# A linear-attention block in front of a feed-forward block: another order and another place of the sums for the products that make keys, values and queries

## The chip, the cores and the metric

The kernel runs on one core of a Trainium2 chip. The metric is the device time of one execution in microseconds (us). PE is TensorE (matmuls), DVE is VectorE, ACT is ScalarE, POOL is GpSimd, and SP is the engine whose queue issues all transfers (DMA) of this kernel. Each engine works through its own instructions in order and stops at the first one whose inputs or buffers are not ready.

## The reference

All arrays are float32: 2048 tokens (S), width 576 (D), 32 heads of 18 channels, feed-forward width 4608.

```python
xn = layernorm(x)                                   # per token, no weights
q, k, v = split(xn @ wqkv)                          # per head: 18 channels each
phi = lambda t: where(t > 0, t + 1, exp(t)) + 1e-6
pq, pk = phi(q), phi(k)
kv = einsum("bhsd,bhse->bhde", pk, v)               # one 18 x 18 state per head
z  = einsum("bhsd->bhd", pk)
num = einsum("bhqd,bhde->bhqe", pq, kv)
den = einsum("bhqd,bhd->bhq", pq, z)[..., None] + 1e-6
s = (num / den) @ wo
g = silu(gelu(xn @ w1 + b1) @ w2 + b2)
out = x + s * g
```

## The kernel before

**Precision.** Float32 products are made of three matmuls each on a pair of parts: a *high* part (a cast, on ACT) and a *low* part (the number minus its high part, on DVE or POOL): high times high, high times low, low times high.

**Tiles and pairs.** The tokens are 16 tiles of 128; two tiles make a pair p, 0 to 7. In the transposed x, a pair and its contraction halves form a 2 x 2 block matrix, and so do the weights of q, k, v. Seven products of sums of blocks (numbered 1 to 7, `product_x`, matmuls at L344) replace the eight plain block products; a rest of the contraction (`REST_OF`) is added to four of them. One product writes 2 x 432 columns (288 for keys or values and 144 for queries in each half) in a double bank of PSUM (`bank2`; there are three of them).

**Start.** The first four tiles are normalized and transposed on PE. Pair 0 is made by four plain products, one for each tile and column half (`plain_x`: 14 steps of two matmuls). The raw weights come in ten loads; their casts (`split_w`, L302 and L303) and the four sums of weight blocks that the seven products need (`w_sum`, L310: T3, T2 and T4 on POOL, T1 on DVE; casts at L315 and L319) are spread over the work of pairs 0 and 1. From pair 2 on, x arrives already transposed from memory (`load_xt`), the token statistics are broadcast through memory (`share_stats`, `load_stats`), POOL subtracts the means (`center`, L239), DVE scales (`scale`, L243) and adds blocks (`x_sums`, L249 to L254), ACT casts (`x_hi_ops`, L257) and DVE makes low parts (`x_lo_ops`, L261). The operands of all pairs are also stored in memory (`store_ops`, tensor `x_dram`, L275) for the feed-forward part.

**Pairs 1 to 7** (`phase1_pair`, `pair`, `evict`). The products run in the order 1, 2, 6, 7, 5, 4, 3. Product 1 is copied to `u` by ACT (L731); 6 is added to it by DVE (L734), 7 is added to that into a second `u` (L736), and the results of 5, 4 and 3 are each added to one of the two (L396, L403, L746). Product 2 accumulates on top of product 1, and 3 on top of 5. The keys go through `phi_hi` (three ACT passes, L373 to L375) and `phi_max` (one DVE pass, L378), and so do the queries of the pair before. `state(p - 1)` (L418) adds the pair before to the sums over tokens, ten matmuls after product 1. Work for the next pairs hangs on the products as hooks (`after1`, `after2`, ...). For the last two pairs only keys and values are made first (N = 288); their queries follow (`pair(..., "q")`), because the final state is then needed sooner.

**Rounds.** Operands of the feed-forward weights are prepared once and stored: five rounds of `we` and nine of `w2`. A round loads, then sums on POOL (L452 and L453, L482), casts on ACT (L459, L486), makes low parts on DVE (L463, L490), stores, and loads the next one. `whole_round` does it in one go: one in each of pairs 2 to 5, two in each of pairs 6 and 7, and one in each of the first turns of attention.

**Attention.** `wo` is folded into the state (`fold_wo`, L958). Then a loop over 16 query tiles, in order `TO`: sums with POOL (L907), denominators on DVE (L914 to L918), the quotient on POOL (L922), a transpose on PE (L1011), a cast, and 28 matmuls (`attend`, L1066). Beside it, x is read back from `x_dram` for the first half of the tokens (`load_x_part`, L1273, four transfers for each segment).

**Feed-forward.** Eighteen steps, nine for each half of the tokens (L1378, L1517). In the last step of the first half, x of the second half is loaded (`load_x_next`).

Engines follow the written order of the program from the first tile to the end of attention (`in_order`).

Of the kernel before, what the change touches and what calls it, by code (L numbers as in the profile page):

```python
# [15 lines left out]
P = 128  # L16
S = 2048
D = 576
# [29 lines left out]
def linear_attention_gated_ffn(ctx, tc, x, xT, wqkv, wo, w1, w1e, b1, w2, b2, out):  # L48
# [52 lines left out]
    b1c = pers.tile([P, NF], F32, name="b1c")  # L101
    nhalf = cst.tile([P, 1], F32, name="nhalf")
    nc.gpsimd.memset(nhalf, -0.5)
    tiny = cst.tile([P, 1], F32, name="tiny")
    nc.gpsimd.memset(tiny, 1e-6)
# [4 lines left out]
    x_dram = dram.tile([2, QH, P, 28, P], F32, name="x_dram")  # L110
# [38 lines left out]
    ORDER_X = (1, 2, 6, 7, 5, 4, 3)  # L149
# [34 lines left out]

    def statistics(t):
# [3 lines left out]
        mv = t0.tile([P, 4], F32, tag="mv", name=f"mv{t}", bufs=4)  # L189
        nc.vector.bn_aggr(mv[:, 0:2], st)  # L190
        nc.vector.tensor_scalar_add(mv[:, 2:3], mv[:, 1:2], 1e-5)
        nc.gpsimd.tensor_tensor(mv[:, 1:2], mv[:, 2:3], nhalf, op=ALU.pow)
        stats[t] = mv
# [80 lines left out]
    def store_ops(p):  # L274
        nc.sync.dma_start(x_dram[p // QH, p % QH], OPS[p].bitcast(F32))  # L275
# [70 lines left out]
    def product_x(p, i, ps, part, first):  # L346
# [4 lines left out]
        if i in REST_OF:  # L351
            r, n = REST_OF[i]
            seq += [(XR[p][:, r], t[:, n]) for t in W["R"]]
        for n, (st, mv) in enumerate(seq):
            mm(ps, st, mv, part, first and n == 0, n == len(seq) - 1)

    def plain_x(j, n, ps, order):

        hi = ((10, 11, 12, 13), (2, 3, 0, 1))[j]
        for i, s in enumerate(order):  # L360
            k = int(s[2])
            if k == 4:
                st = XR[0][:, (REST_T0, REST_T1)[j]]
            else:
                st = OPS[0][:, hi[k] + XLO * (s[0] == "l")]
            mm(ps, st, w_plain(k, n)[s[1] == "l"], "all", i == 0, i == len(order) - 1)
# [45 lines left out]
    def state(p):  # L412
        if not ps_kv:
            ps_kv.extend((bank1("ps_kva"), bank1("ps_kvb")))
        for j in (1, 0):
# [7 lines left out]

    def phi_k1_hi(p):
        phi_hi(f"k{p}1", as2(k_bufs[1]))

    def phi_k1_max(p):
        phi_max(f"k{p}1", k_bufs[1], as2(k_bufs[1]))
# [12 lines left out]
    class W2Round:  # L441
# [9 lines left out]
        def sums(self):  # L451
            nc.gpsimd.tensor_tensor(self.src[5][0], self.src[5][1], self.src[5][0], op=SUB)  # L452
            nc.gpsimd.tensor_tensor(self.src[6][0], self.src[6][0], self.src[6][1], op=SUB)  # L453
# [16 lines left out]
    class WeRound:  # L470
# [8 lines left out]
        def sums(self):  # L479
            u = self.u  # L480
            for dst, a, b in ((4, 0, 1), (5, 3, 0), (6, 3, 4), (7, 2, 6)):
                nc.gpsimd.tensor_tensor(u[:, dst], u[:, a], u[:, b], op=SUB)  # L482
# [25 lines left out]
    def round_sums():  # L508
        loaded[0].sums()
# [11 lines left out]
    def whole_round():  # L521
        if loaded:
            round_sums(), round_hi(), round_lo(), round_store()

# [5 lines left out]
    xn_all = opp.tile([P, 4 * KT * P], F32, tag="OPS", name="xn")  # L530
    r_tile(0), op_tiles(0), r_tile(1)
    for t in range(4):
        xn[t] = xn_all[:, t * KT * P : (t + 1) * KT * P]
# [8 lines left out]
    load_x(3)  # L542
# [5 lines left out]
    def transpose_into(t, places):  # L548
        for k, dst in enumerate(places):
            nc.tensor.transpose(dst, xn[t][:, k * P : (k + 1) * P], ident)  # L550

    def slots(ps, n=4):
        return ps[:, : n * P].rearrange("p (k c) -> p k c", k=n)

    FIRST = "hh0 hh1 lh0 lh1 hl0 hh2 lh2 hl1 hh3 lh3 hl2 hh4 hl3 hl4".split()
    LATER = "hh2 lh2 hl2 hh3 lh3 hl3 hh0 lh0 hl0 hh1 lh1 hl1 hh4 hl4".split()
    assert sorted(FIRST) == sorted(LATER)
    dve, pool = nc.vector, nc.gpsimd

    statistics(0)  # L560
    normalize_dve(0)
    split_w(0, 0, dve)
    split_w(1, 0, pool)

    ta, tb = bank1("pt0a"), bank1("pt0b")
    a4, b1_ = slots(ta), slots(tb, 1)[:, 0]
    transpose_into(0, [a4[:, k] for k in range(4)] + [b1_])
    o0, xr0 = OPS[0], XR[0]
    nc.scalar.copy(xr0[:, REST_T0], b1_)
    for k in (slice(0, 2), slice(2, 4)):  # L570
        h, l = o0[:, 10 + k.start : 10 + k.stop], o0[:, 24 + k.start : 24 + k.stop]
        nc.vector.tensor_copy(h, a4[:, k])
        nc.vector.tensor_tensor(l, a4[:, k], h.bitcast(F32), op=SUB)
    nc.vector.tensor_tensor(
        xr0[64:, REST_T0], b1_[64:], xr0[64:, REST_T0].bitcast(F32), op=SUB
    )
    split_w(2, 0, pool)
    split_w(3, 0, dve)
    split_w(4, 0, dve)
    statistics(1)  # L580
    offset(1)
    xa = bank2("x00")
    plain_x(0, 0, xa, FIRST)
    normalize_act(1)

    pt1 = bank2("pt1")
    c4, d1 = slots(pt1[:, 0]), slots(pt1[:, 1], 1)[:, 0]
    transpose_into(1, [c4[:, 2], c4[:, 3], c4[:, 0], c4[:, 1], d1])
    split_w(2, 1, dve)
    split_w(3, 1, dve)  # L590
    nc.scalar.copy(o0[:, 0:4], c4)
    nc.scalar.copy(xr0[:, REST_T1], d1)
    nc.vector.tensor_tensor(o0[:, 14:18], c4, o0[:, 0:4].bitcast(F32), op=SUB)
    nc.vector.tensor_tensor(
        xr0[64:, REST_T1], d1[64:], xr0[64:, REST_T1].bitcast(F32), op=SUB
    )
    xc = bank2("x02")
    plain_x(1, 0, xc, FIRST)
    statistics(2)
    offset(2)  # L600
    q_tile(0)
    phi_hi("k00", kv_of(xa))
    copy_q(0, 0, xa)
    phi_max("k00", k_bufs[0], kv_of(xa))
    normalize_act(2)
    nc.scalar.copy(R[0][:, 13:17], a4)
    nc.scalar.copy(R[0][:, 17], b1_)
    split_w(0, 1, dve)
    split_w(1, 1, dve)
    split_w(4, 1, dve)  # L610
    load_x(4), load_x(5)

    def transpose_to_r(t):
        pa, pb = bank1(f"pt{t}a"), bank1(f"pt{t}b")
        if t % 2:
            a, b = slots(pa, 3), slots(pb, 2)
            transpose_into(t, [a[:, 0], a[:, 1], b[:, 0], b[:, 1], a[:, 2]])
            return (R[1][:, 0:3], a), (R[1][:, 3:5], b)
        a, b = slots(pa), slots(pb, 1)
        transpose_into(t, [a[:, k] for k in range(4)] + [b[:, 0]])  # L620
        return (R[1][:, 13:17], a), (R[1][:, 17:18], b)

    to_r = transpose_to_r(2)
    statistics(3)
    offset(3)
    w_sum("T3", 0, pool), w_sum("T3", 1, pool)
    for dst, src in to_r:
        nc.scalar.copy(dst, src)
    normalize_act(3)
    xa = bank2("x01")  # L630
    plain_x(1, 1, xa, LATER)

    q_tile(1)
    phi_hi("k01", kv_of(xc))
    copy_q(1, 0, xc)
    phi_max("k01", k_bufs[1], kv_of(xc))
    memset_v()
    nc.scalar.copy(R[0][:, 3:5], c4[:, 0:2])
    nc.scalar.copy(R[0][:, 0:2], c4[:, 2:4])
    nc.scalar.copy(R[0][:, 2], d1)  # L640
    w_sum("T1", 0, dve), w_sum("T1", 1, dve)
    for k in range(2):
        w_sum("T2", k, pool), w_sum("T4", k, pool)
    x_sums(0, rest=False)
    store_rest(0)
    to_r = transpose_to_r(3)
    for dst, src in to_r:
# [1250 lines left out]
```

## Time and profile before

| | |
|---|---|
| two runs | 1268.87 and 1269.29 us, median 1269.08 |
| the profiled execution | 1267.1 us, of it the span of the profile 1265.4 |
| PE busy | 1129.8 us (89%) in 6480 matmuls |
| DVE busy | 856.0 us (68%) |
| ACT busy | 502.8 us (40%) |
| POOL busy | 481.9 us (38%) |
| mean granted clock of PE | 0.932 |
| transfers | 284.94 MB in 120784 packets, mean 225 GB/s |

The span runs from the first to the last instruction. The granted clock is the share of full speed that PE was given. A wait in brackets, "[12.43 <-DVE kph L378]", is the idle time of the engine ahead of an instruction, and what ended it: an instruction by its engine, the tile that it writes, and its line. A timeline row gives start, length, engine, line, operation, output<-inputs, sizes and count.

### The profile page before, as it was taken

The numbers are of one execution on the slowest core, as the hardware profiler recorded it, in microseconds if no ns is written. First come the engines' busy times: TensorE is split into PE (matmuls) and PEld (weight loads), VectorE is DVE, ScalarE is ACT, GpSimd is POOL, SyncE is SP. The second block draws the span as 40 slices with busy tenths as digits, with TensorE's granted clock in tenths as the row PEclk, the third lists the DMA queues.
The fourth block names the chain that finished last, engine by engine and source line by source line (L and its number), as shares of the span: only waits on it lengthen the run. The fifth ranks groups of instructions, "written<-read, shape, count | busy, mean of one in ns | idle before, by whom it ended". The sixth has DMA issues, their size and how long they took to land.

```text
span 1265.4 us, 17904 instructions
## 1 busy us (share of the span) xinstructions
PE 1129.8 (89%) x6480; PEld 1034.5 (82%) x6480; DVE 856.0 (68%) x1221; ACT 502.8 (40%) x835; POOL 481.9 (38%) x410
## 2 busy tenths in 40 slices
PE   8687998556558599999999999979999999999998
PEld 7577897555557588998998998878999899899888
DVE  6856776236445188888888888875576567557666
ACT  5543554234223154455445445425234223323333
POOL 2423222213454254455545445533134223423430
PEclk8688898777778799999999999999999999999999
DMA  5256655423789996568568657799776667777552
GB/s 197 83 206 202 210 180 230 163 70 101 238 269 298 308 375 244 189 263 297 209 217 319 221 191 283 252 303 380 264 258 208 223 204 241 231 215 234 165 158 105
DMA packets 120784, 284.94 MB, mean 225 GB/s; under 512 B 13558, under 2 KB 55542, under 8 KB 118136
## 3 DMA queue, kind: packets, MB, share of 16 engines
q1 hardware_dynamic: 120696, 283.80, 65.7%
q8 instruction: 51, 0.84, 0.3%
q14 instruction: 37, 0.30, 0.1%
HBM read 176.23 MB, written 106.64 MB: 224 GB/s over the span
## 4 chain that ended last, share of the span: by engine, by line
PE 65%; DMA 6%; SPq 3%; DVE 3%; ACT 2%; POOL 1%; issue 1%; POOLq 0%; DVEq 0%; ACTq 0%
PE pm L1517 29%; PE zy L1378 9%; PE e L1378 9%; PE a L1378 9%; PE b L1378 5%; PE pd L1637 2%; DMA w2r<-w 1%; SPq L1273 1%; PE xq L344 1%; DMA q<-q_dram 1%; PE ps_s L1066 1%; DMA rq_dram<-wa_rest0s 1%; DMA rxm<-rq_dram 1%; DMA we<-we_dram 0%; PE ps_kw L958 0%
## 5 line engine op out<-in xcount | busy, mean ns | idle before, releaser
L1523 DVE TENSOR_TENSOR macc<-pm,macc 128x576 f32<-128x576 f32 x218 | 163.9, 752 | 49.9 <-PE pm L1517 48.4
L1101 ACT CAST h_h<-g 128x512 fp32r<-128x512 f32 x204 | 121.8, 621 | 132.7 <-PE pm L1517 131.7
L1104 DVE TENSOR_TENSOR h_l<-g,h_h 128x512 fp32r<-128x512 f32 x204 | 161.8, 800 | 0.0
L1483 POOL TENSOR_TENSOR mid<-g 128x512 f32<-128x512 f32 x34 | 43.9, 1291 | 120.2 <-ACT g L1386 120.2
L1477 POOL TENSOR_TENSOR g<-g 128x512 f32<-128x512 f32 x34 | 54.9, 1615 | 50.1 <-DVE h_l L1104 28.2
L1386 ACT ACTIVATE g<-b,b1c 128x512 f32<-128x512 f32 x36 | 24.9, 690 | 105.3 <-DVE b L1404 105.3
L1395 ACT COPY mid<-a 128x512 f32<-128x512 f32 x36 | 21.1, 585 | 111.1 <-PE a L1378 111.1
L1398 DVE TENSOR_TENSOR mid<-b,mid 128x512 f32<-128x512 f32 x36 | 24.8, 690 | 55.0 <-PE b L1378 52.2
L1147 POOL TENSOR_TENSOR w1raw<-w1raw 128x256 f32<-128x256 f32 x18 | 13.2, 736 | 124.9 <-ACT h_h L1101 68.2
L463 DVE TENSOR_TENSOR w2o<-w2r,w2o 128x576 fp32r<-128x576 f32 x18 | 24.1, 1337 | 53.7 <-ACT w2o L459 52.6
L1480 POOL TENSOR_TENSOR g<-g 128x512 f32<-128x512 f32 x34 | 55.2, 1623 | 2.7
L1066 PE MATMUL ps_s<-kw_h,th 128*128 128x288 f32 x160 | 42.6, 354 | 13.4 <-ACT kw_h L1054 7.0
L1608 POOL TENSOR_TENSOR fin1l<-fin1h,fin1l 128x288 f32<-128x288 f32 x8 | 7.0, 875 | 118.8 <-DMA fin1l<-s_dram 55.5
L1378 PE MATMUL a<-h0r,wa 128*128 128x512 f32 x144 | 50.4, 390 | 0.0
L1378 PE MATMUL a<-h0f,wa 128*128 128x512 f32 x144 | 50.4, 390 | 0.0
L1104 DVE TENSOR_TENSOR h_l<-mid,h_h 128x512 fp32r<-128x512 f32 x34 | 48.8, 1435 | 1.2
L418 PE MATMUL ps_kva<-kph,vb 128*127 128x126 f32 x128 | 26.1, 368 | 25.6 <-DVE kph L378 21.2
L1011 PE MATMUL ptp<-ident,vb 128*128 128x128 f32 x80 | 15.8, 338 | 34.5 <-ACT s L1071 22.4
L418 PEld LDWEIGHTS ps_kva<-kph,vb 128*127 128x127 f32 x128 | 23.2, 271 | 27.8 <-DVE kph L378 23.2
L1386 ACT ACTIVATE g<-e,b1c 128x512 f32<-128x512 f32 x36 | 24.8, 689 | 51.2 <-DVE e L1411 51.2
L1474 POOL TENSOR_TENSOR g<-g 128x512 f32<-128x512 f32 x34 | 44.0, 1295 | 2.7
L1066 PEld LDWEIGHTS ps_s<-kw_h,th 128*128 128x128 f32 x160 | 31.8, 234 | 16.1 <-ACT kw_h L1054 7.4
(998 smaller groups left out, 3715.3 us busy)
## 6 DMA issues: line engine op xcount, KB each, us to landing
we<-we_dram SPq DMA_DIRECT2D x36, 448.0 KB, 6.0
x_dram<-OPS SPq DMA_DIRECT2D x8, 1792.0 KB
w2raw<-w SPq DMA_DIRECT2D x10, 1152.0 KB
op<-w2o SPq DMA_DIRECT2D x18, 576.0 KB, 3.9
w1raw<-w SPq DMA_DIRECT2D x18, 512.0 KB, 5.8
op_a<-wa SPq DMA_DIRECT2D x18, 512.0 KB, 5.5
op_c<-wc SPq DMA_DIRECT2D x18, 512.0 KB, 4.1
op_d<-wd SPq DMA_DIRECT2D x18, 512.0 KB, 5.6
```

The costliest lines, as they stand in the source:

```text
L418: nc.tensor.matmul(dst, v_bufs[j][:, i, : G + 1], k_bufs[j][:, g : g + n], start=(p == 0 and j == 1 and i in (0, 4)), stop=(p == NPR - 1 a ...
L1066: nc.tensor.matmul(ps[:, h, :HD], st[:, k, :], w[:, k, h * HD : (h + 1) * HD], start=(i == 0), stop=(i == len(seq) - 1),)
L1101: nc.scalar.copy(pair[0], src)
L1104: eng.tensor_tensor(pair[1], src, pair[0].bitcast(F32), op=SUB)
L1378: nc.tensor.matmul(ps, st, mv, start=first and n == 0, stop=n == len(seq) - 1, skip_group_check=True,)
L1386: nc.scalar.activation(g, ps, AF.Gelu_apprx_tanh, bias=b1c[:, f : f + 1])
L1474: tt(src[5, pr], A(1, 0), A(1, 1), op=ADD)
L1477: tt(src[6, pr], src[5, pr], A(0, 0), op=SUB)
L1480: tt(src[3, pr], A(0, 1), src[6, pr], op=SUB)
L1483: tt(src[7, pr], A(0, 0), A(1, 0), op=SUB)
L1517: nc.tensor.matmul(ps[:, q, :HD], hs[p][st][:, cs], m[:, p, :], start=(n == 0 and i not in CHAIN), stop=(n == 5), skip_group_check=True,)
L1523: nc.vector.tensor_tensor(dst, src, dst, op=ADD)
```

## The change

- **Pair 1 is plain too:** pairs 0 and 1 are made by four plain products each (`plain_x` takes the pair), and the seven products start with pair 2. The first four tiles go from their transposes straight to operands. Queries of tiles 0 to 3 are stored without phi, which is applied in attention (`RAW`). All weight sums are on POOL.
- **Four products in one tile:** the order is 2, 1, 6, 7, 5, 4, 3. Products 1, 6, 7 and 4 accumulate in one PSUM tile A; ACT copies A after 1, 6 and 7 (`snapshot`). The DVE additions into `u` are gone. The rest products of 2 and 5 are steps of their own (`e2`, `e5`), and the state of the pair before is split in two halves (`sa`, `sb`) between the products. T1's keys and queries come out of A without an addition; those of T0 now need one.
- **Rounds:** one in each of pairs 3 to 7 and one in the queries of pair 6, with sums, casts, low parts and store on different hooks. In attention a round takes two turns: sums, now on DVE, at the end of an even turn, the rest at the end of the next. Six rounds lie ahead of attention (eight before) and eight in it (six before).
- **x by partition:** `x_dram` holds 512 tokens in a row for each partition and segment. A pair stores 512-byte pieces; a segment is read in one transfer instead of four.
- **Around the state:** phi of the first two query tiles, the fold and the first denominators hang on other products of the last part; phi of the last two query tiles moves into the second turn of attention; a copy (`zb`) moves from ACT to POOL.

```diff
-    x_dram = dram.tile([2, QH, P, 28, P], F32, name="x_dram")
+    x_dram = dram.tile([2, P, 28, 512], F32, name="x_dram")
...
-    ORDER_X = (1, 2, 6, 7, 5, 4, 3)
+    ORDER_X = (2, 1, "e2", "sa", 6, "sb", "e5", 7, 5, 4, 3)
...
     def store_ops(p):
-        nc.sync.dma_start(x_dram[p // QH, p % QH], OPS[p].bitcast(F32))
+        cs = slice(p % QH * P, (p % QH + 1) * P)
+        nc.sync.dma_start(x_dram[p // QH, :, :, cs], OPS[p].bitcast(F32))
...
+    x10 = bank2("x10")
+    plain_x(1, 0, 0, x10, THEN[:10], last=False)
+    transpose_x(3)
+    plain_x(1, 0, 0, x10, THEN[10:], first=False)
...
+    w_sum("T4", 0, pool), w_sum("T4", 1, pool)
+    k10 = phi_plain(2, x10)
+    state(0)
+    x12 = bank2("x12")
+    plain_x(1, 1, 0, x12, THEN)
+    k10()
+    scale(2)
+    x_sums(2)
+    w_hi("T2", 0), w_hi("T2", 1)
+    w_lo("T2", 0, dve), w_lo("T2", 1, dve)
...
+    x13 = bank2("x13")
+    plain_x(1, 1, 1, x13, THEN)
...
+    x11 = bank2("x11")
+    plain_x(1, 0, 1, x11, THEN)
...
-        elif i == 6:
-            u = u_part(u1, part)
-            nc.vector.tensor_tensor(u, ps_part(ps, part), u, op=ADD)
-        elif i == 7:
-            nc.vector.tensor_tensor(
-                u_part(u2, part), ps_part(ps, part), u_part(u1, part), op=ADD
-            )
...
+    def snapshot(p, n, ps, part):
+        nc.scalar.copy(u_part(u_all[p][n], part), ps_part(ps, part))
+
+    def products(p, part, hooks, before=None):
...
+        for i in ORDER_X:
+            if i == 2:
+                X0 = bank2(f"x0{part}{p}")
+                product_x(p, 2, X0, part, True, rest=False)
+            elif i == 1:
+                A = bank2(f"xa{part}{p}")
+                product_x(p, 1, A, part, True)
+                snapshot(p, 0, A, part)
+            elif i == "e2":
+                rest_alone(p, 2, X0, part, False)
+            elif i in ("sa", "sb"):
+                if before is not None:
+                    state(before, (1,) if i == "sa" else (0,))
+            elif i == 6:
+                product_x(p, 6, A, part, False, rest=False)
+                snapshot(p, 1, A, part)
+            elif i == "e5":
+                X1 = bank2(f"x1{part}{p}")
+                rest_alone(p, 5, X1, part, True)
+                u = u_all[p][0]
+                if kv:
+                    nc.vector.tensor_tensor(
+                        as2(k_bufs[0]), kv_of(X0), as2(u)[:, :, :KV], op=ADD
+                    )
+                    phi_hi(f"k{p}0", as2(k_bufs[0]))
+                if q:
+                    add_q(T0, 0, X0, u, part)
+            elif i == 7:
+                product_x(p, 7, A, part, False, rest=False)
+                snapshot(p, 0, A, part)
+                if kv:
+                    phi_max(f"k{p}0", k_bufs[0], as2(k_bufs[0]))
+            elif i == 5:
+                product_x(p, 5, X1, part, False, rest=False)
+                if kv:
+                    add_v(1, X1, u_all[p][0])
+                if q:
+                    add_q(T1, 1, X1, u_all[p][0], part)
+            elif i == 4:
+                product_x(p, 4, A, part, False)
+                if kv:
+                    phi_hi(f"k{p}1", kv_of(A))
+                if q:
+                    copy_q(T1, 0, A, part)
+            else:
+                product_x(p, 3, X1, part, False)
+                def end():
+                    if kv:
+                        phi_max(f"k{p}1", k_bufs[1], kv_of(A))
+                        add_v(0, X1, u_all[p][1])
+                    if q:
+                        add_q(T0, 1, X1, u_all[p][1], part)
+                pend.append(end)
             hooks.get(i, lambda: None)()
...
-    ROUND_OF = {2: 1, 3: 1, 4: 1, 5: 1, 6: 2, 7: 2}
...
+        def h1():
+            if steady:
+                operands_hi()
...
+            if p in ROUNDS:
+                round_sums()
...
+        def hsb():
+            if steady:
+                operands_lo()
+            if first:
+                w_hi("T4", 0), w_hi("T4", 1)
+                w_lo("T4", 0, pool), w_lo("T4", 1, pool)
+                center(3)
+            if p in ROUNDS:
+                round_hi()
...
+        def h7():
+            if nxt and not first:
+                center(nxt)
+            if first:
+                operands()
+                operands_hi()
+            if p in ROUNDS:
+                round_lo(), round_store()
...
-    pair(NPR - 2, "q", {})
+    products(NPR - 2, "q", {2: round_sums, 7: lambda: (round_hi(), round_lo(), round_store())})
...
         for a, n, to in X_SEGS[k]:
-            for c in range(QH):
-                nc.sync.dma_start(
-                    t[:, to : to + n, c * P : (c + 1) * P].bitcast(F32),
-                    x_dram[half, c, :, a : a + n],
-                )
+            nc.sync.dma_start(t[:, to : to + n].bitcast(F32), x_dram[half, :, a : a + n])
...
         if j + 4 < NT:
+            if TO[j + 4] in RAW:
+                phi_q_hi(TO[j + 4]), phi_q_max(TO[j + 4])
             by_sums(j + 4)
             denominators(j + 4)
             p_mult(j + 4)
+        if j == 1:
+            for t in TO[-2:]:
+                phi_q_hi(t), phi_q_max(t), store_q(t)
         beside(j)
-        if j < 9 and loaded:
-            whole_round()
+        if loaded and j % 2 == 0:
+            round_sums(dve)
+        elif loaded:
+            round_hi(), round_lo(), round_store()
```

More of the change, by code (lines that the diff above doesn't have):

```diff
@@ L344, in mm, with product_x @@
             nc.tensor.matmul(dst, st, w, start=start, stop=stop, skip_group_check=True)
-    def product_x(p, i, ps, part, first):
+    def product_x(p, i, ps, part, first, rest=True):
         (wh, wl), a, o = W[W_OF[i]], X_OF[i], OPS[p]
@@ L561, in linear_attention_gated_ffn @@
     normalize_dve(0)
-    split_w(0, 0, dve)
+    split_w(0, 0, pool)
+    transpose_x(0)
     split_w(1, 0, pool)
[L565 to L573, printed above, removed]
@@ new lines, in linear_attention_gated_ffn @@
+    for k in (2, 3, 4):
+        if k == 2:
+            statistics(1)
+        split_w(k, 0, dve)
+        if k == 2:
+            offset(1)
+    x00 = bank2("x00")
+    plain_x(0, 0, 0, x00, FIRST[:12], last=False)
+    normalize(1)
+    transpose_x(1)
+    plain_x(0, 0, 0, x00, FIRST[12:], first=False)
+    ones_of_v()
+    statistics(2), offset(2)
+    tile_hi(1)
+    tile_lo(1)
+    split_w(2, 1, dve), split_w(3, 1, dve)
+    x02 = bank2("x02")
+    plain_x(0, 1, 0, x02, THEN)
+    k00 = phi_plain(0, x00)
```

456 lines of the change are left out of this document (225 added, 231 removed).

## The prediction

> **What bounds the kernel now.** I read the page, then one table of stretches, then the waits of PE, then the timeline round the gaps.
>
> ```profile
> span 1265.4 us, 17904 instructions
> 0.00:45.00 45.00, 35.37 (x152) 31.82 (x153) 29.30 (x43) 22.96 (x41) 19.40 (x23) 0.85 0.38 140
> 45.00:85.00 40.00, 29.11 (x121) 26.59 (x120) 28.78 (x51) 19.87 (x29) 10.59 (x8) 0.74 0.50 185
> 85.00:121.00 36.00, 27.31 (x125) 25.29 (x124) 21.06 (x40) 12.87 (x19) 10.57 (x12) 0.81 0.54 171
> 121.00:195.00 74.00, 69.42 (x359) 64.72 (x358) 53.48 (x102) 38.05 (x55) 22.02 (x20) 0.95 0.65 221
> 195.00:249.00 54.00, 37.04 (x244) 36.32 (x243) 24.84 (x39) 19.84 (x28) 11.65 (x28) 0.81 0.46 168
> 249.00:290.00 41.00, 25.10 (x141) 22.65 (x140) 13.00 (x25) 12.34 (x23) 5.58 (x4) 0.79 0.29 92
> 290.00:304.00 14.00, 4.74 (x22) 2.82 (x20) 9.89 (x19) 8.61 (x17) 6.22 (x5) 0.69 0.26 85
> 304.00:380.00 76.00, 48.12 (x259) 44.03 (x258) 38.81 (x53) 18.44 (x36) 36.65 (x28) 0.77 0.71 235
> 380.00:442.00 62.00, 42.99 (x265) 40.91 (x265) 23.77 (x44) 15.51 (x31) 20.65 (x17) 0.81 0.95 303
> 442.00:826.00 384.00, 383.47 (x2246) 348.28 (x2247) 332.74 (x433) 185.45 (x321) 201.19 (x163) 1.00 0.71 256
> 826.00:854.00 28.00, 21.02 (x151) 20.35 (x151) 20.08 (x25) 7.65 (x11) 8.50 (x6) 0.96 1.05 296
> 854.00:1265.00 411.00, 406.09 (x2412) 370.71 (x2411) 260.19 (x353) 141.25 (x228) 128.91 (x100) 0.99 0.68 222
> ```
>
> The columns are the stretch, its length, the busy time of PE, PE's weight loads, DVE, ACT and POOL, the granted clock, the DMA share and GB/s. I cut the table where the kernel changes work: plain products of pair 0 until 45, pair 1 until 85, pair 2 until 121, pairs 3 to 5 until 195, keys and values of pairs 6 and 7 until 249, their queries until 290, the start of attention, attention until 442, then the feed-forward part. From 442 on PE is full but for 826 to 854, so only the first 442 us and that one hole can shrink. There PE is idle about a quarter of the time, and the clock is low wherever it is idle.
>
> ```profile
> PE ps_kva L418 <- DVE kph L378: 21.2, 6, 12.4
> PE xq L344 <- ACT u L731: 15.9, 2, 11.3
> PE ptp L1011 <- ACT s L1071: 22.4, 5, 6.5
> 232.92 2.07 PE L418 MATMUL ps_kva<-kph,vb 128*127 128x126 f32 x8 [12.43 <-DVE kph L378]
> 261.19 0.61 PE L344 MATMUL xq<-wB21h,OPS 128*128 128x288 f32 x1 [11.28 <-ACT u L731]
> 276.55 0.61 PE L344 MATMUL xq<-wB21h,OPS 128*128 128x288 f32 x1 [4.62 <-ACT u L731]
> 224.80 1.40 POOL L452 TENSOR_TENSOR w2r<-w2r 128x576 f32<-128x576 f32 x1 [20.34 <-DMA w2r<-w]
> ```
>
> The waits (total, times, longest) have one source behind several names. A round of w2 is done in one go: POOL waits for the load, then ACT, DVE and the store follow, and each engine stops in order. POOL starts a sum the moment its load lands (224.80), PE resumes at 232.92; 11.28 and the waits for s in attention are the same picture.
>
> **The change part by part.** First the prices.
>
> ```profile
> 8.08 2.78 PE L344 MATMUL x<-wB11h,OPS 128*128 128x432 f32 x8 [1.38 <-DVE OPS L572]
> 123.92 1.15 PE L418 MATMUL ps_kva<-kph,vb 128*127 128x126 f32 x8 [0.64 <-DVE kph L378]
> 126.16 0.64 PE L344 MATMUL xall<-wB21h,OPS 128*128 128x432 f32 x2
> 129.38 0.56 PE L344 MATMUL xall<-wT2h,OPS 128*128 128x432 f32 x2
> 131.75 0.56 PE L344 MATMUL xall<-wT3h,OPS 128*128 128x432 f32 x2
> 239.43 0.43 PE L344 MATMUL xkv<-wT2h,OPS 128*128 128x288 f32 x2
> 241.02 0.43 PE L344 MATMUL xkv<-wT3h,OPS 128*128 128x288 f32 x2
> 125.05 0.88 ACT L731 COPY u<-xall 128x864 f32<-128x864 f32 x1 [1.98 <-DVE q L403]
> 132.25 1.05 DVE L734 TENSOR_TENSOR u<-xall,u 128x864 f32<-128x864 f32 x1
> 37.81 9.32 POOL L310 TENSOR_TENSOR raw<-raw,raw 128x864 f32<-128x864 f32 x4 [2.00 <-DVE raw L310]
> 40.91 2.15 DVE L250 TENSOR_TENSOR R<-R 128x256 f32<-128x256 f32 x1
> 126.92 0.43 DVE L250 TENSOR_TENSOR R<-R 128x256 f32<-128x256 f32 x1
> 273.87 0.68 ACT L373 ACTIVATE eq<-q 128x576 f32<-128x576 f32 x1
> ```
>
> Twelve matmuls take 131.75 − 129.38 = 2.37 us, 0.1975 each; keys and values alone 1.59, 0.1325 each; the state's ten 126.16 − 123.92 = 2.24.
>
> *Start.* Pair 1 is now plain: 8 products of 28 matmuls, 224 × 0.1975 = 44.2, with one state 46.5. At the clock of the first stretch, 0.85, that is 54.7; the first product starts at 8.1, which makes 63. I add 8 of waits: PE was idle 45 − 35.4 = 9.6 before. All eight sums of weights lie on POOL now (9.32 / 4 = 2.33 each, 18.6) beside the sums of x on DVE, which take 2.15 there and 0.43 with POOL free. So pair 2 starts at 71 instead of 85: **−14**. Bounds: 55 (full clock, no wait) and 85.
>
> *Pair 2* takes over the weights' casts, and what it hands to pair 3 goes through POOL twice (low parts of T4, then centering) before DVE may scale. Floor 100 × 0.1975 + 2.24 = 22; pair 1 with this work took 40. I take 31, near the middle, against the 36 of today's pair 2: **−5**.
>
> *Pairs 3 to 5.* DVE loses two adds of 1.05, ACT gains two copies of 0.88 (busy 38.05 of 74 now). The copy is a new wait: PE may not go on in that bank before it, and queued behind it on ACT are the operand casts, for which DVE's low parts wait. Rest products and half of the state, 0.8 + 1.1 = 1.9 us, lie between; they cover 0.88 if ACT comes in time. Floor 3 × 22 = 66, now 74 with PE busy 69.4. I take 72: **−2**; bounds 66 and 80.
>
> *Pairs 6 and 7.* Floor 2 × (13.25 + 2.24) = 31, now 54. One round per pair, its sums, casts and store in three places, loses the 12.4 and most of the rest of 21.2. I take 37: **−17**; bounds 31 and 54.
>
> *Queries of 6 and 7.* Both waits, 11.28 + 4.62, are for a copy behind other ACT work; the first goes with the round, but the exponentials of two query tiles now stand ahead of copies of pair 7, as today. I take **−10**; bounds 0 and −16. *290 to 304* keeps its chain of casts: 0, with ±2.
>
> *Attention.* Rounds are split over two turns, so POOL and PE stop less. But DMA was busy 0.71 × 76 + 0.95 × 62 = 113 us of the 138, and two rounds more fall into this stretch.
>
> ```profile
> x_dram<-OPS SPq DMA_DIRECT2D x8, 1792.0 KB
> op<-w2o SPq DMA_DIRECT2D x18, 576.0 KB, 3.9
> w2r<-w SPq DMA_DIRECT2D x9, 864.0 KB, 6.4
> we_dram<-weo SPq DMA_DIRECT2D x5, 896.0 KB, 4.5
> 825.00:850.00 25.00, 21.64 (x158) 20.97 (x156) 20.32 (x26) 7.65 (x11) 9.50 (x6) 1.00 1.06 281
> 850.00:855.00 5.00, 1.38 (x3) 1.16 (x4) 0.00 (x0) 0.55 (x2) 0.00 (x0) 0.67 1.01 406
> 853.62 0.80 PE L1378 MATMUL a<-rxm,we 128*128 128x512 f32 x1 [6.98 <-DMA we<-we_dram]
> ```
>
> One round of each kind is about 864 + 2 × 576 + 896 KB and a small load, 3.2 MB, 8 us at 406 GB/s. Against it, half of x, 4 × 1792 KB = 7.3 MB, is read in long rows instead of 512-byte pieces: 25 to 27 us at the 281 GB/s of 825 to 850, where such pieces run, 18 at 406. The two cancel; 113 at a share of 0.95 is 119. I take 122: **−16**; bounds 113 and 138 + 8 = 146. The exponentials of query tiles 0 to 3 move here, and those of the last two, with their stores, from ahead of attention into its second turn. Each is three ACT passes of 0.68, so 2 us; they cost nothing while ACT is busy only 18.44 of 76. Without that cover it would be 12. On SP the round's stores and its next load now stand behind a turn's load of x and ahead of the next turn's store of s; a late round would hold that store, and with it the next load of queries.
>
> The Trainium skill, DMA: Bandwidth & Descriptors, section Specifications, puts the smallest transfer at line rate at 512 B. By it the new layout would bring no speed, only fewer issues, and the attention term would be −8. The trace differs: both windows above are full, at 281 and 406.
>
> *Half change.* At 853.62 PE has waited 6.98 for a load queued behind x. 7 MB (281 GB/s for 25 us) land about 8 us sooner at 406, and ten issues replace forty on SP: **−7**; bounds 0 and −9. The price stands in the stores, now 512-byte rows: 8 × 1.8 MB, 2 us more each, 16 in all, hidden while the DMA share stays at 0.65 and below until 290; 16 if that cover were gone.
>
> Sum: 14 + 5 + 2 + 17 + 10 + 16 + 7 = 71. The profiled execution took 1267.1 (its span plus 1.7); 1267.1 − 71 = 1196.1. It lies 2 under the median of the runs, 1269.08, so I say **1198**.
>
> **The rivals.**
>
> *Snapshots stop PE (slower).* 24 copies (three in each of pairs 2 to 7 and of the two query parts), each as late as the one at 276.55, cost 24 × 4.62 = 111: 1309. It eats the gain from 71 / 24 = 3 us each on. For it: both long waits of xq are for just this copy. Against: ACT is half idle, and in pairs 3 to 5 no such wait is among PE's longest.
>
> *Attention stays as it is.* DMA is full from 380 on and gets the rounds too: 1198 + 16 + 8 = 1222. For it: a share of 0.95; against: 76 us at 0.71 ahead of it.
>
> *The lock holds the start.* DVE's sums last 2.15 beside POOL's 2.33: each waits for the other. If DVE, not PE, then paces the plain products, 14 are lost, 1212. The Trainium skill, SBUF — State Buffer, section Who interferes with whom, says that a VectorE instruction with two SBUF inputs and a GpSimd one that reads SBUF exclude each other for the whole instruction. The rows agree.
>
> *Rounds still stop the engines,* because loads land no sooner: the 24 of 12.4 + 11.3 and attention's 16 stay: 1238.
>
> *PE runs at its floor:* start 63, pair 2 at 25, pairs 6 and 7 at 32, attention 115: 8 + 6 + 5 + 7 = 26 less, 1172.
>
> **How the numbers follow.** Forecast 0.46; floor 0.14; attention unchanged 0.14; lock 0.12; rounds 0.07; snapshots 0.07. The forecast and the four cases next to it lie between 1165 and 1250 with their spread, which leaves some 0.15 outside, so the range is 1165 to 1250. A change of under 2%, 1244 to 1294, is about what a measurement here cannot tell from none. Faster by more: 0.87, from the forecast, the floor, attention, the lock and half of the rounds; within 2%: 0.07; slower: 0.06, the snapshots.
>
> **What would show it.** In the changed profile: pair 2's first product at about 71, pair 3's at about 102; the queries done by about 242; no PE wait over 5 us for a state's keys or for a copy; attention about 122 long, its DMA share over 0.9 throughout; no 7 us wait after the half change, and x loads over 350 GB/s. It is wrong if PE's waits for u grow to 3 us per snapshot, if pair 2 starts after 80, or if attention stays at 138.

## The result, and the profile after

The changed kernel takes 1228.8 us (median of 1228.32 and 1229.29) against 1269.08: a ratio of 0.9683, 95% interval 0.9641 to 0.9724. It is faster, by 40 us where the prediction said 71; the time lies inside the stated range of 1165 to 1250, 31 us above the forecast of 1198. The profiled execution took 1229.29 us, 1227.6 of it the span.

First the table of stretches, cut where the stages of the changed kernel begin (columns as in the prediction: stretch, length, PE, weight loads, DVE, ACT, POOL, granted clock, DMA share, GB/s).

```profile
span 1227.6 us, 17832 instructions
0.00:73.00 73.00, 57.47 (x284) 51.03 (x284) 47.14 (x75) 35.22 (x65) 33.21 (x30) 0.93 0.48 153
73.00:107.60 34.60, 25.91 (x120) 24.18 (x121) 22.80 (x39) 16.10 (x24) 7.69 (x5) 0.80 0.62 192
107.60:187.40 79.80, 68.03 (x362) 64.39 (x361) 48.81 (x98) 43.15 (x61) 27.28 (x25) 0.91 0.71 209
187.40:223.70 36.30, 32.98 (x242) 32.58 (x241) 19.36 (x31) 20.28 (x30) 9.17 (x23) 0.95 0.66 217
223.70:269.30 45.60, 27.64 (x160) 22.94 (x158) 19.68 (x41) 18.53 (x39) 13.75 (x11) 0.87 0.31 102
269.30:330.00 60.70, 46.87 (x297) 44.66 (x297) 36.23 (x63) 26.79 (x48) 21.69 (x15) 0.87 0.57 183
330.00:404.00 74.00, 36.95 (x221) 36.33 (x222) 34.73 (x50) 14.11 (x27) 15.84 (x12) 0.72 0.95 350
404.00:420.00 16.00, 10.02 (x37) 7.19 (x35) 10.20 (x13) 6.57 (x12) 4.61 (x5) 0.82 0.88 322
790.00:830.00 40.00, 40.00 (x247) 36.87 (x246) 31.53 (x41) 19.57 (x27) 12.97 (x8) 1.00 1.02 398
```

The stages, side by side with the kernel before. There, attention begins at 303.6 and the feed-forward part at 433.1, where it waits 7.9 us in its first steps; it has one more gap of 7 us at the half change. Here it starts at 404.0 and waits 7.2 us in its first steps. These first waits are counted with attention, which so ends at 441.0 and at 411.2.

| stage | before | after | difference | forecast |
|---|---|---|---|---|
| to pair 2's first product | 85.0 | 73.0 | -12.0 | -14 |
| pair 2 | 36.0 | 34.6 | -1.4 | -5 |
| pairs 3 to 5 | 74.0 | 79.8 | **+5.8** | -2 |
| keys and values of 6 and 7 | 54.0 | 36.3 | -17.7 | -17 |
| queries, state, fold | 54.6 | 45.6 | -9.0 | -10 |
| attention | 137.4 | 141.9 | **+4.5** | -16 |
| feed-forward | 824.4 | 816.4 | -8.0 | -7 |
| span | 1265.4 | 1227.6 | -37.8 | -71 |

Five of seven terms are within 4 us. Two have the wrong sign, and the waits of PE say where (waited for: total, times, longest):

```profile
PE ps_s L1175 <- DVE th L1130: 45.8, 8, 14.3
PE xaall L361 <- ACT u L800: 11.8, 1, 11.8
PE ps_s L1175 <- ACT kw_h L1163: 10.7, 1, 10.7
PE x1all L361 <- DVE q L428: 8.6, 1, 8.6
PE x0all L361 <- DVE kph L403: 6.7, 1, 6.7
PE a L1493 <- ACT mid L1510: 5.7, 1, 5.7
```

The largest is new: in attention PE waits for a low part from DVE. The page's list of groups tells what DVE itself waited for; this group's idle time, 49.7 us, is all for one kind of load:

```profile
L471 DVE TENSOR_TENSOR w2r<-w2r 128x576 f32<-128x576 f32 x6 | 4.5, 758 | 49.7 <-DMA w2r<-w 49.7
```

The sums of a round, now on DVE, are queued one turn behind the issue of their load. DVE reaches them first and stops, and the low part of the next query tile is behind them. The three longest of PE's waits for it, 14.3, 12.5 and 9.7 us, follow such stops.

The 11.8 us in pair 3 name a snapshot, but the snapshot is the last link. The timeline, one row for each engine from the back:

```profile
130.47 1.09 PE L361 MATMUL xaall<-wT3h,OPS 128*128 128x432 f32 x2 [11.77 <-ACT u L800]
127.96 1.68 ACT L273 CAST OPS<-R 128x1792 fp32r<-128x1792 f32 x1
121.97 0.82 DVE L259 TENSOR_TENSOR R<-R,bc 128x640 f32<-128x640 f32 x1 [12.66 <-POOL R L255]
120.38 3.82 POOL L255 TENSOR_TENSOR R<-R,bc 128x640 f32<-128x640 f32 x2 [12.22 <-DMA bc<-st_dram]
107.61 0.55 POOL L187 TENSOR_TENSOR mv<-mv,nhalf 128x1 f32<-128x1 f32 x1 [0.61 <-DVE mv L186]
```

Read upwards: the statistics of pair 4 are finished on POOL at 108.2; their way through memory ends at 120.38; centering, scaling and the operand cast follow, and the copy of A (129.55) is queued behind that cast on ACT.

### The profile page after: what moved, and what is told of

The parts are those of the page before. It is cut to its first block, busy times and chain, and to the rows that moved or that the text cites. A ratio compares the mean times of both kernels' runs of the same rounds, so it can differ in the third digit from the quotient of the medians.

```text
span 1227.6 us, 17832 instructions
## 1 busy us (share of the span) xinstructions
PE 1107.6 (90%) x6492; PEld 1015.6 (83%) x6492; DVE 847.6 (69%) x1212; ACT 512.9 (42%) x858; POOL 470.5 (38%) x391
## 4 chain that ended last, share of the span: by engine, by line
PE 65%; DMA 6%; DVE 3%; issue 2%; SPq 1%; ACT 0%; POOL 0%; DVEq 0%; ACTq 0%
PE pm L1632 31%; PE e L1493 9%; PE zy L1493 9%; PE a L1493 9%; PE b L1493 5%; DMA w2r<-w 3%; PE pd L1752 2%; DMA s_dram<-s 1%; DVE w2o L482 1%; DMA rq_dram<-wa_rest1s 0%; DMA wa_rest1q<-rr_dram 0%; DMA we<-w1e 0%; DVE den L1017 0%; DVE w2r L471 0%; DVE w2r L472 0%
## 5 line engine op out<-in xcount | busy, mean ns | idle before, releaser
L1175 PE MATMUL ps_s<-kw_h,th 128*128 128x288 f32 x160 | 41.3, 345 | 56.5 <-DVE th L1130 45.8
L1592 POOL TENSOR_TENSOR g<-g 128x512 f32<-128x512 f32 x34 | 54.9, 1615 | 49.7 <-DVE h_l L1213 28.4
L1513 DVE TENSOR_TENSOR mid<-b,mid 128x512 f32<-128x512 f32 x36 | 24.8, 690 | 45.6 <-PE b L1493 39.8
L1025 POOL TENSOR_TENSOR vb<-q,den 128x576 f32<-128x576 f32 x14 | 19.3, 1377 | 74.9 <-DVE den L1021 64.6
L1589 POOL TENSOR_TENSOR g<-g 128x512 f32<-128x512 f32 x34 | 44.2, 1299 | 2.7
L1526 DVE TENSOR_TENSOR e<-e,mid 128x512 f32<-128x512 f32 x36 | 24.8, 690 | 22.3 <-PE e L1493 22.3
L1175 PE MATMUL ps_s<-kw_l,th 128*128 128x288 f32 x160 | 39.6, 334 | 0.0
L471 DVE TENSOR_TENSOR w2r<-w2r 128x576 f32<-128x576 f32 x6 | 4.5, 758 | 49.7 <-DMA w2r<-w 49.7
```

Of the source, the lines that this page charges most:

```text
L1175: nc.tensor.matmul(ps[:, h, :HD], st[:, k, :], w[:, k, h * HD : (h + 1) * HD], start=(i == 0), stop=(i == len(seq) - 1),)
L1513: tt(u1_sb, B, m1_sb, op=ADD)
L1589: tt(src[5, pr], A(1, 0), A(1, 1), op=ADD)
L1592: tt(src[6, pr], src[5, pr], A(0, 0), op=SUB)
```

## The experiments

Each was timed beside the kernel before, whose median was 1269.8 to 1271.6 in these runs.

| run | median us | ratio to before, 95% interval |
|---|---|---|
| e1 statistics early | 1218.2 | 0.9588, 0.9564 to 0.9611 |
| e2 sums late | 1220.2 | 0.9597, 0.9567 to 0.9627 |
| e3 rounds in one go | 1247.3 | 0.9815, 0.9793 to 0.9838 |
| e4 before, new layout alone | 1255.0 | 0.9881, 0.9858 to 0.9904 |
| e5 e2 and x early | 1215.8 | 0.9567, 0.9539 to 0.9594 |
| e6 exponentials, x load | 1223.7 | 0.9633, 0.9609 to 0.9656 |
| e7 T4 on DVE | 1225.4 | 0.9648, 0.9630 to 0.9665 |
| e8 two rounds in a pair | 1256.4 | 0.9894, 0.9874 to 0.9914 |
| e9 e2 and two buffers | 1215.9 | 0.9565, 0.9550 to 0.9579 |
| e10 e1, snapshots twice | 1221.5 | 0.9609, 0.9595 to 0.9623 |
| e11 together | 1198.3 | 0.9428, 0.9412 to 0.9444 |
| e12 together and x early | 1188.6 | 0.9341, 0.9317 to 0.9365 |

**e1, statistics early.**

```diff
         def h7():
             if first:
+                next_statistics()
                 operands()
...
         def h5():
             if first:
                 rest_lo(prep), operands_lo()
-                next_statistics()
```

> The changed kernel with one thing moved: the statistics of tiles 8 and 9 (pair 4) in pair 2 stand ahead of pair 3's operands, not behind their low parts and store. Theory (late statistics): in the changed kernel's trace DVE makes them at 105.1, their broadcast lands at 120.4, POOL's centering, DVE's scaling and sums and ACT's cast of the operands follow, and the snapshot queues behind that cast until PE has waited 11.8 us at 130.5. DVE was idle from 90.3 to 96.4. Made there, the broadcast lands about 105, the wait falls under 2 us, pair 3 takes 24 instead of 36 and the whole 1217 to 1220. Rival (the snapshot itself is too much for ACT beside the casts): the wait stays above 8 and the time at 1227 to 1229. Rival (the broadcast is held by the transfers ahead of it): half the wait stays, 1223.

1218.2 us, as the theory had it. POOL's centering of pair 4, from this run's timeline, then the issues on SP in the changed kernel (two rows) and in this run (two rows):

```profile
97.24 1.86 POOL L187 TENSOR_TENSOR mv<-mv,nhalf 128x1 f32<-128x1 f32 x2
105.44 1.58 POOL L255 TENSOR_TENSOR R<-R,bc 128x640 f32<-128x640 f32 x1 [6.34 <-DMA bc<-st_dram]
105.28 0.52 SPq L292 DMA_DIRECT2D x_dram<-OPS  x1
107.03 4.82 SPq L232 DMA_DIRECT2D st_dram<-mv  x2
98.39 1.15 SPq L232 DMA_DIRECT2D st_dram<-mv  x2
105.27 0.54 SPq L292 DMA_DIRECT2D x_dram<-OPS  x1
```

PE's wait of 11.8 us for the copy is gone and pairs 3 to 5 take 67.2 us (106.6 to 173.8), 1.2 over the floor of 66. The late statistics were the cause, not the snapshot. The way through memory also shrank, from 12.2 to 6.3: the store of 1.8 MB of operands no longer stands ahead of it on SP.

**e2, sums late.**

```diff
-        if loaded and j % 2 == 0:
-            round_sums(dve)
-        elif loaded:
-            round_hi(), round_lo(), round_store()
+        if loaded and j % 2:
+            round_sums(dve), round_hi(), round_lo(), round_store()
```

> The changed kernel with attention's round sums (still on DVE) at the end of the odd turn, directly ahead of the casts, so that the load has two turns instead of one. Theory (DVE stops for the load): DVE waited 52 us for loads of rounds in attention and PE 45 us for th behind it; loads take 6 to 11 us, two turns some 15. DVE's waits for w2r fall under 15 us in all, PE's for th under 20, attention (first product of it to the first of the feed-forward part, 134.7) to about 120, the whole to 1212 to 1218. Rival (transfers bound attention, share 0.82 and 0.96): the wait moves to other loads, attention stays above 130 and the time within 4 us of 1229.

1220.2 us, between the theory's range and the rival's. Attention takes 124.0 (270.4 to 394.4), 10.7 less, where the theory gave 14.7. The waits of PE, then of DVE, then the stretches:

```profile
PE ptp L1124 <- ACT s L1180: 37.1, 6, 12.7
PE ps_s L1175 <- DVE th L1130: 3.1, 3, 2.1
DVE w2r L471 <- DMA w2r<-w: 31.1, 5, 10.3
270.00:330.00 60.00, 46.87 (x299) 44.53 (x300) 38.69 (x66) 26.84 (x49) 20.74 (x15) 0.84 0.59 186
330.00:394.00 64.00, 36.06 (x218) 34.16 (x218) 31.76 (x48) 13.84 (x27) 18.07 (x14) 0.76 1.01 380
```

The wait for th fell from 45.8 to 3.1, and most of it came back under another name: ACT, waiting with a cast for DVE's sums, holds the copy of s. Two turns are still too short for the load; from 330 on the transfers are full.

**e3, rounds in one go.**

```diff
             if p in ROUNDS:
-                round_lo(), round_store()
+                round_sums(), round_hi(), round_lo(), round_store()
```

(and no other part of a round on other hooks)

> The changed kernel with each round of pairs 3 to 7 and of pair 6's queries done in one go after product 7 (sums, casts, low parts, store), still one for each. Theory (what helped pairs 6 and 7 is one round for each pair, so that its load has a whole pair's time): no more than 3 us lost, 1228 to 1232. Rival (what helped is the spreading over three places): each of six rounds stops ACT and DVE for a cast's and a sum's length, 2 to 5 us each, 1239 to 1255, with a wait for u behind product 7 in every pair.

1247.3 us, in the rival's range, but both were half right. Pairs 6 and 7 take 35.9 us (207.2 to 243.1), as with the spread; pairs 3 to 5 take 101.5 (105.7 to 207.2) instead of 79.8. The waits of PE and POOL:

```profile
PE x1all L361 <- DVE q L428: 22.7, 4, 8.0
POOL R L255 <- DMA bc<-st_dram: 32.3, 5, 10.9
```

At hook 7 a round's sums stand behind the centering on POOL, which waits for its broadcast; pairs 6 and 7 have no pair to prepare, or only one without centering there. By this trace, spreading pays there because it takes the sums out from behind that wait; no run moves the sums alone.

**e4, the new layout alone,** put into the kernel before: the three pieces of the diff that name `x_dram`.

> The kernel before with the new layout of x_dram alone (512 tokens in a row for each partition; stores in 512-byte pieces, one transfer for each segment read). Theory (as in the prediction): the 7 us wait after the half change goes, attention gains 0 to 5 where its x loads end, stores cost nothing: 1257 to 1263. Rival (stores in pieces delay what is queued behind them in pairs 1 to 5): the gain is eaten, 1266 to 1275.

1255.0 us, 14.8 less than before: more than either expected. Of the feed-forward part one wait of PE is left, against two before (7.9 and 7.0, the second after the half change):

```profile
PE a L1375 <- DMA rxm<-rq_dram: 5.2, 1, 5.2
```

Attention up to there takes 124.0 (307.8 to 431.8) instead of 129.5, and from there to the end 820.4 instead of 832.3. Ahead of attention 4.2 us are lost. So in these two profiles the layout brings about 17 and costs 4.

**e5, x early,** on top of e2.

```diff
-    FIRST_AT = {5: "h0", 6: "l0", 7: "s2", 8: "h1", 9: "l1", 10: "s1", 11: "s4"}
+    FIRST_AT = {0: "l0", 1: "l1", 2: "s1", 3: "s4", 5: "h0", 6: "s2", 7: "h1"}
```

> The sums-late kernel with the seven loads of x for the feed-forward part in other turns of attention: those without a rest (l0, l1, s1, s4) in turns 0 to 3, h0 in 5, s2 in 6, h1 in 7, instead of turns 5 to 11. Theory (with the sums late, transfers are the bound, but only from 330 on: share 1.00 and 1.02 at 330 to 405, 0.58 at 269 to 330): about 4 MB move into the slack, 10 us at 400 GB/s; DVE's waits for w2r, 31 us there, fall below 15; attention, 124 there, takes about 114, the whole 1208 to 1213 against 1220. Rival (SP's order is the bound: loads of x ahead of the stores of s and the loads of q): the early turns lengthen as much as the late ones shrink, 1217 to 1225.

1215.8 us, between the two ranges and within the scatter of e2; attention takes 123.6 (269.7 to 393.3), not 114. Its stretches and DVE's wait:

```profile
269.00:300.00 31.00, 22.13 (x137) 21.02 (x138) 16.31 (x30) 18.19 (x31) 6.87 (x5) 0.78 0.43 142
300.00:393.00 93.00, 63.34 (x381) 60.23 (x380) 54.77 (x85) 23.38 (x46) 31.83 (x24) 0.80 0.94 339
DVE w2r L471 <- DMA w2r<-w: 28.3, 5, 9.5
```

From 330 on the transfers are no longer quite full (a share of 0.91, against 1.01 in e2), and still the loads come late. A second limit would explain it: with one buffer a load is issued only when the round before it has been stored. That is what e9 tests.

**e6, two moves in stages far apart.**

```diff
     def f4():
+        phi_q_hi(TO[2]), phi_q_max(TO[2])
         folds(2)
+        phi_q_hi(TO[3]), phi_q_max(TO[3])
...
     transpose_p(0)
-    phi_q_hi(TO[2]), phi_q_max(TO[2])
...
     transpose_p(1)
-    phi_q_hi(TO[3]), phi_q_max(TO[3])
...
-                sums_plain_lo(1)
-                load_xt(3), load_xt(4)
+                x_lo_ops(1, 2, 10)
+                load_xt(3)
+                store_ops(1)
+                load_xt(4)
```

> The changed kernel with two things moved, in stages far apart. (a) The exponentials of the two stored query tiles that come third and fourth in attention move from behind the first two transposes into the last product of the queries. Theory: attention's first cast of the folded state waits 7.2 us at 268.6 for POOL's copy, which ends a chain of exponentials, maxima, sums and quotients; two exponentials and maxima of 2.9 us each leave it, so the first product of attention comes 4 to 6 us after the queries sooner. Rival: POOL's four long passes set it, under 2 us. (b) In pair 2 the transposed x of pair 3 is loaded ahead of the store of pair 1's operands. Theory: the load, issued at 84.2 behind 1.8 MB of 512-byte pieces, lands 4 us sooner than 94.8, and PE's wait of 8.7 us at 102.2 falls to 5. Rival: the landing is bound by the load's own small packets and moves under 1 us. Both theories 1218 to 1221, both rivals 1227 to 1229.

1223.7 us. The first two rows are of the start of attention (POOL's third quotient and ACT's first cast), the last two of POOL's centering of pair 3, in the changed kernel and then in this one:

```profile
256.51 1.16 POOL L1027 TENSOR_TENSOR vb<-OPS,den 128x576 f32<-128x576 f32 x1 [6.51 <-DVE den L1023]
262.36 0.67 ACT L1165 CAST kw_h<-kw 128x576 fp32r<-128x576 f32 x1 [7.04 <-POOL zb L1145]
94.79 3.06 POOL L255 TENSOR_TENSOR R<-R,bc 128x640 f32<-128x640 f32 x2 [5.14 <-DMA R<-xT]
90.11 3.65 POOL L255 TENSOR_TENSOR R<-R,bc 128x640 f32<-128x640 f32 x2
```

(a) goes to the rival by its size: the cast still waits 7.04, and from the queries to attention it takes 44.2 instead of 45.6. But POOL's passes alone do not set it: POOL stands idle for 6.51 us until the denominators come from DVE, where they are queued behind the last steps of the queries and the low parts of the first transpose; the copy `zb` ends a chain that goes back and forth between the two engines. (b) goes to the theory: the wait for the load is gone, the centering starts 4.7 sooner, and pair 2 takes 30.0 instead of 34.6. The store does have a price: what is queued behind it.

**e7, T4's sums on DVE.**

```diff
-    w_sum("T4", 0, pool), w_sum("T4", 1, pool)
...
     w_lo("T3", 0, dve), w_lo("T3", 1, dve)
+    w_sum("T4", 0, dve), w_sum("T4", 1, dve)
```

> The changed kernel with the two sums of T4 on DVE behind T3's low parts, not on POOL beside pair 2's scaling. Theory (the two engines hold each other up): scaling and the first sum of pair 2's x took 4.79 and 2.11 us beside POOL, 1.6 and 0.4 are left; the keys' maximum queued behind them on DVE comes 5 us sooner, PE's wait of 6.7 us falls to 2 and pair 2 starts about 68.5 instead of 73.0; two sums of 1 us each on DVE are hidden in pair 2: 1224. Rival (the pair's start is bound by the casts and not by this): start at 72 to 73, 1228.

1225.4 us; pair 2 starts at 68.3, as the theory had it. POOL's sums of T4 in the changed kernel with DVE's scaling and first sum beside them, then DVE's two rows in this run:

```profile
63.50 5.19 POOL L327 TENSOR_TENSOR raw<-raw,raw 128x864 f32<-128x864 f32 x2
62.03 4.79 DVE L259 TENSOR_TENSOR R<-R,bc 128x640 f32<-128x640 f32 x2 [1.48 <-POOL R L255]
66.85 2.11 DVE L265 TENSOR_TENSOR R<-R 128x256 f32<-128x256 f32 x1
```

```profile
60.85 2.93 DVE L259 TENSOR_TENSOR R<-R,bc 128x640 f32<-128x640 f32 x2 [1.50 <-POOL R L255]
63.81 0.43 DVE L265 TENSOR_TENSOR R<-R 128x256 f32<-128x256 f32 x1
```

The scaling did not fall to the 1.6 expected: POOL's centering (59.22 to 62.36) still runs beside its first half.

**e8, rounds as before.**

```diff
-            if p in ROUNDS:
-                round_lo(), round_store()
+            for _ in range(ROUND_OF.get(p, 0)):
+                round_sums(), round_hi(), round_lo(), round_store()
...
-    ROUNDS = range(3, NPR)
+    ROUND_OF = {3: 1, 4: 1, 5: 1, 6: 2, 7: 2}
```

> The changed kernel with rounds as they were before: in one go, one in each of pairs 3 to 5 and two in each of pairs 6 and 7, none in the queries. What is read from it are pairs 6 and 7. Theory (the second round of a pair waits for a load that is issued only when the first has been stored): their keys and values take 46 to 54 us, with waits of over 8 us behind POOL's w2r as in the kernel before; with one round in each they took 36.3 and, in one go, 36.2. Rival (the new order of products, not the rounds, made them short): 36 to 40. Pairs 3 to 5 lose about 21 to rounds behind the centering on POOL, as with one round in one go; the whole 1250 to 1262 by the theory, 1242 to 1248 by the rival.

1256.4 us, in the theory's range. Pairs 6 and 7 take 59.6 (207.6 to 267.2), even more than in the kernel before. PE's wait, and POOL's at a second round:

```profile
PE x1kv L361 <- DVE vb L421: 20.5, 2, 11.1
231.13 1.81 POOL L501 TENSOR_TENSOR we<-we 128x128 f32<-128x128 f32 x4 [18.96 <-DMA we<-w1e]
```

The new order of products alone saves nothing there; one round for each pair does.

**e9, a second buffer,** on top of e2.

```diff
+    raw_pools = [tw]
+    def raw_pool():
+        raw_pools.append(raw_pools.pop(0))
+        return raw_pools[-1]
...
-            t = tw.tile([P, 3, 2, HD], F32, tag="raw", name=f"w2r{self.c}", bufs=1)
+            t = raw_pool().tile([P, 3, 2, HD], F32, tag="raw", name=f"w2r{self.c}", bufs=1)
...
+    raw_pools.insert(0, ph2.enter_context(tc.tile_pool(name="rw2", bufs=1, side="right", reuse_waits="tile")))
+    round_load()
     load_q(4), load_q(5)
```

> The sums-late kernel with a second buffer for the raw weights of a round in attention, so that a load is under way while the round before it is worked on. Theory (rounds in attention are a serial chain: a load is issued only when the round before it has been stored, comes 7 to 10 us later, and only then sums, casts and low parts follow; with the x loads moved away attention stayed at 123.6, and DVE's waits for w2r at 28): DVE's waits for w2r fall below 10 us, attention from 124 to 110 to 116, the whole to 1206 to 1212. Rival (transfers are the bound, share 1.00 from 330 to 380): the waits move to the loads of q, x or the stores; attention stays above 120, 1216 to 1222.

1215.9 us, attention 120.0 (270.0 to 390.0): the rival, at its lower edge. ACT's wait (23.6 of it in attention) and the last stretch:

```profile
ACT w2o L484 <- DMA op<-w2o: 31.5, 7, 14.5
330.00:390.00 60.00, 34.02 (x215) 31.72 (x214) 31.68 (x45) 14.18 (x27) 17.36 (x14) 0.80 1.00 378
```

The load is early now, and DVE no longer waits for it; the wait stands at the stores of the round before.

**e10, every snapshot twice,** on top of e1.

```diff
-        nc.scalar.copy(u_part(u_all[p][n], part), ps_part(ps, part))
+        for _ in range(2):
+            nc.scalar.copy(u_part(u_all[p][n], part), ps_part(ps, part))
```

> The stats-early kernel with every snapshot copied twice by ACT (the same copy again; 24 more copies, 18 of 0.88 or 0.64 us with keys, six of 0.40 for queries alone). Theory (a snapshot is hidden by the rest products and the half state behind it): no more than 5 us, 1216 to 1223, pairs 4 and 5 stay within 1 us each. Rival (each copy stands in PE's path): about 18 us, 1234 to 1238, each pair longer by 2 to 2.6.

1221.5 us, in the theory's range: 3.3 more than e1, at the edge of the scatter, for some 17 us of copies. Pairs 4 and 5 take 23.8 and 22.5 against 23.0 and 22.0. The snapshots are mostly hidden.

**e11, together:** e1, e2, e6, e7 and the buffer of e9.

> The changed kernel with the statistics early, the sums late and the second raw buffer in attention, the exponentials and the x load of the earlier run moved, and T4's sums on DVE. Theory (the waits lie one after another in different stages, so what they gave alone adds up: 11, 9, 5 and 3.5, and 8 to 13 for the buffer): 1187 to 1194. Rival (attention is bound by transfers, so what comes earlier into it waits there): stages ahead of attention keep their 20, attention stays at 124, 1199 to 1207.

1198.3 us, 0.7 below the rival's range and 4 above the theory's. Ahead of attention 18.9 us are won (269.3 to 250.4), attention takes 123.0 (to 373.4), as in e2: there the gains do not add up.

**e12, e11 with the x loads of e5.**

> The kernel with everything together and, beside it, the x loads of the feed-forward part in turns 0 to 7 of attention. Theory (two things bound attention one after the other: the chain of a round with one raw buffer, and from 330 on the transfers; each taken away alone gave 4 us or nothing, since the other was left; at 269 to 300 the share was 0.34 with two buffers): with both away attention falls from 123 to 108 to 115, the whole to 1184 to 1191. Rival (the sums, casts and stores of rounds between the steps of attention bound it in any case): 120 or more, 1194 to 1200.

1188.6 us, inside the theory's range; this version beats both kernels. But the number came without its mechanism: in the profiled execution, which at 1191.1 is the slowest of its four, attention takes 119.0 (250.2 to 369.2), more than the 108 to 115 expected:

```profile
250.00:280.00 30.00, 21.64 (x136) 20.54 (x137) 16.12 (x29) 17.65 (x31) 6.88 (x5) 0.78 0.44 144
280.00:369.00 89.00, 61.49 (x383) 58.25 (x382) 55.45 (x87) 24.11 (x47) 32.33 (x24) 0.83 0.98 358
ACT w2o L484 <- DMA op<-w2o: 20.5, 6, 8.0
```

From 280 to 369 the transfers are full, so that bound was not taken away. Whether fewer rounds in attention, more of them earlier, would shorten it was not tried; that stays open.

## Why the prediction was right or wrong

**Attention (forecast -16, measured +4.5)** is the step that failed: "Rounds are split over two turns, so POOL and PE stop less". Splitting a round does not help if its first part still comes too early for its load. The load has one turn, and a stop of DVE holds each turn's low part, for which PE waits 45.8 us in all. That POOL would have been the better engine to stop is argued and not shown: no run has the split with the sums on POOL. The rival "rounds still stop the engines, because loads land no sooner" came true here, and only here; the rival nearest in time, attention unchanged at 1222, gave full transfers as its reason. The prediction looked at shares and bytes and did not ask, as it should for a moved wait, what is queued behind it. With the sums a turn later (e2) the term would have been 124.0 plus the first feed-forward waits of 7.7, some 132: about -6, still far from the forecast. The other half, that the DMA share is over 0.9 "throughout", was wrong in place: it is 0.57 until 330 and 0.95 after, so the slack lies at the beginning.

**Pairs 3 to 5 (-2, +5.8).** The working had the operand casts queued behind the copy on ACT, and its bound of 80 holds the 79.8. In pair 3 it is the other way round: the copy is queued behind the cast, and the cast is late by the statistics of pair 4, whose new place behind pair 3's operands and behind the operand store on SP was not followed. Without it the term is 67.2 (e1), -6.8, better than forecast.

**Pair 2 (-5, -1.4)** was mis-sized by a price set to zero, the stores of x: 4.6 us (e6) come back when the next load goes ahead of one. Bandwidth was hidden, as stated; the place on the queue was not.

**The start (-14, -12.0)** had pair 2 at 71, measured 73.0. The rival of the lock was there in small: 4.7 us by e7. The Trainium skill, SBUF — State Buffer, section Who interferes with whom, says that a VectorE instruction with two SBUF inputs and a GpSimd one that reads SBUF exclude each other. The rows of e7 agree: 2.11 us against 0.43 for the same sum.

**Pairs 6 and 7 (-17, -17.7)** and **the queries (-10, -9.0)** were right in size. For pairs 6 and 7 the cause is narrower than told: not that a round is split but that each pair has one (e3, e8). For the queries no run shows the cause by itself: in e8, with two rounds in pair 7, they take 41.5 us (267.2 to 308.7), less than in the changed kernel. The gain there does not hang on spreading the rounds, whose stop in e8 lies ahead of the queries. The exponentials of the two stored tiles moved in e6 cost under 2 us there, though PE's wait for kw_h did grow from 7.0 to 10.7: it stands at the end of the chain of denominators, quotients and the copy `zb`, which came over from ACT to POOL.

**The half change (-7, -8.0)** and the speed of long rows were right: 398 GB/s from 790 to 830, no wait. But weighing rounds against layout to zero in attention hid a gain: with the layout alone (e4) attention is 5.4 us shorter and its first feed-forward wait 2.7, and the changed kernel shows next to none of it.

**Snapshots stop PE** did not happen: 3.3 us for 24 copies more (e10). The sign that no PE wait of over 5 us should be for a copy pointed at the wrong thing, since the 11.8 us bear the copy's name and have another cause.

**The chances.** The parts named for "faster by more" add up to 0.895, not 0.87; nothing else hangs on it.

## What to carry to other kernels

When work that waits for a load is moved, move it behind the time that the load needs, and choose the engine by what is queued behind it: here a stop of POOL became a stop of DVE, and with it of PE. The engine named at the end of a wait is the last link of a chain; follow it back until you find an idle engine or a transfer, and look there for the edit. When a resource is full only in the second half of a stage, taking away one wait moves it to the next: earlier loads (e5) and a second buffer (e9) gave about 4 us each on top of e2, no more than the scatter of its runs, and the earlier loads 9.7 once the buffer was there (e11 to e12).

## What was not expected of the hardware

- The statistics of two tiles took 12.2 us from POOL through memory and back when a store of 1.8 MB stood ahead on the queue, and 6.3 when it did not.
- Storing x in 512-byte pieces and reading it in long rows brought 14.8 us in a kernel otherwise unchanged; where these reads run at the half change, 281 GB/s were moved with 512-byte pieces and 398 with rows, at a full share in both (from 806 on loads of weights run in the second stretch as well).
- Scaling 2 x 128x640 on DVE took 4.79 us beside POOL's sums and 2.93 without them.
